# Moving the regroup copies of a fused attention and feed-forward kernel from GpSimd to ScalarE, with the sums around them rescheduled

## The chip, the cores and the metric

The kernel runs on one core of a Trainium2 chip. The metric is the device time of one execution in microseconds (us). The engines are named as the profile names them: PE is TensorE (matmuls; PEld is its loading of weights), DVE is VectorE, ACT is ScalarE, POOL is GpSimd, SP is SyncE, which here only starts stores. Each engine works through its own instructions in the order of the program and waits where an operand or a buffer isn't ready.

## What is computed

Linear attention over 8 batches of 8 heads, 576 positions and 64 features, without softmax, then an RMS norm over each head's 64 features, then a feed-forward layer with PReLU over the 4608 tokens of 512 features.

```python
kv  = einsum('bhsd,bhse->bhde', k, v)
out = einsum('bhsd,bhde->bhse', q, kv)
out = out / sqrt(mean(out*out, axis=-1, keepdims=True) + 1e-6) * g_norm
x   = out.transpose(0, 2, 1, 3).reshape(4608, 512)
h   = x @ w_in                                   # 512 -> 2048
g   = maximum(h, 0) + alpha * minimum(h, 0)
y   = g @ w_out                                  # 2048 -> 512
```

## The kernel before

The 4608 tokens are nine windows of 512, w = 0 to 8. Window 0 is worked through alone, its attention first and then its h matmuls. In **stage two** the first three quarters of window 0's output, in the banks ya, yb and yc, are accumulated beside the attention of window 1 (yc only half). After that comes one **block** for each window w from 1 to 8: its h matmuls, the output products of window w - 1, and the attention of window w + 1, in 16 units u = 0 to 15. An **epilogue** computes the products of window 8.

From window 1 on, `g @ w_out` is split into 2 x 2 quarters and done in seven products instead of eight (Strassen's method in Winograd's form). This needs sums of quarters of g (`s_sum`, 16 for each window, on DVE) and of w_out (`w_sum`, 8 in all, on DVE).

```python
def w_sum(n, i):                      # i = 0, 1: half of the rows
    ...
    else:                             # n == 3 overwrites part of w_out itself
        nc.vector.tensor_sub(
            out=w_lo(i, HC, D_MODEL), in0=w_hi(i, HC, D_MODEL), in1=w_lo(i, HC, D_MODEL))

def s_sum(w, n, k):                   # k = 0..3; needs the g groups of both halves
    t = sum_p.tile([P, 2, HW], FP16, name=f"s{n}", tag=f"s{n}{k}", bufs=1 if n == 2 else 2)
    if n == 1:   nc.vector.tensor_add(out=t[:], in0=a21, in1=a22)
    elif n == 2: nc.vector.tensor_sub(out=t[:], in0=sums[w, 1, k][:], in1=a11)
    elif n == 3: nc.vector.tensor_sub(out=t[:], in0=a11, in1=a21)
    else:        nc.vector.tensor_sub(out=t[:], in0=a12, in1=sums[w, 2, k][:])
```

q and k of a batch are loaded into a staging tile (`qst`, `kst`, two buffers each, filled by DMAs that POOL starts) with head outermost. A **regroup** copy puts them into an order (`qsb`, `ksb`, three buffers) in which the 128 columns of a head pair lie together, as PE's weight load reads them. v is read from its staging tile directly.

```python
def regroup(b, nm, h0, h1, eng=None):
    dst = bufs[b % NBUF][nm][:, 0:TPP, h0:h1, :].rearrange("p t h d -> p h t d")
    src = stages[b, nm][:, h0:h1, :, :]
    if eng is nc.scalar: nc.scalar.copy(out=dst, in_=src)
    else: (eng or nc.vector).tensor_copy(out=dst, in_=src)
```

The attention of a window goes by head pair j = 0 to 3 in four steps: `t` transposes q on PE and ACT copies it out (`qt_sb`); `kv` multiplies k and v on PE and DVE copies it out under a mask (`kv_sb`); `ot` multiplies both on PE and ACT squares it (`sq_sb`); `ssq` sums the squares on PE, ACT takes the reciprocal root (`rstd`), and DVE scales the result to `xt`, the input of the h matmuls. From block 1 on, `qt_ps`, `kv_ps` and `ssq_ps` take turns in one PSUM bank, tag "s".

The h matmuls go to two PSUM banks in turn (three before block 1). ACT takes the negative part (`m_sb`), then DVE forms g (`gt`), and only then is the bank free for the second group after it.

```python
def m1_group(w, g):
    h_ps = h_bank()
    m1_mm(h_ps, w, g, range(NC))                 # 4 matmuls of 128 x 512
    # m1_evac:
    nc.scalar.activation(out=m_sb[:], in_=h_ps[:], func=AF.Relu, scale=-1.0)
    nc.vector.scalar_tensor_tensor(out=gts[w, i][:, r, :], in0=m_sb[:],
        scalar=beta_sb[:, g:g+1], in1=h_ps[:], op0=ALU.mult, op1=ALU.add)
```

The block loop:

```python
Y_ORDER = (1, 6, 2, 7, 5, 4, 3)                  # the seven products, 16 matmuls each
PER = 7                                          # products' matmuls in a unit
Y_READS = {2: ("p1",), 5: ("u2",), 7: ("c11",), 9: ("u3",), 12: ("c22",), 14: ("c21",)}

def unit_sums(w, u):
    k, r = divmod(u, 4)
    if k > 0:
        s_sum(w, r + 1, k - 1)                   # 12 in block w, 4 in block w + 1

# t, kv, ot, ssq of pair j at units 3j, 3j + 1, 3j + 3, 3j + 5

for w in range(1, NW):
    shift = 1 if w == 1 else 0
    if w + 2 < B: load_batch(w + 2)
    for u in range(NF):
        m1_group(w, G_ORDER[u])
        unit_sums(w, u)
        if w > 1 and u < 4: unit_sums(w - 1, NF + u)
        if w == 2 and u in (1, 2): w_sum(3, u - 1)
        if w == 1 and u in (1, 3): w_sum(2 if u == 1 else 4, 1)
        if w + 2 < B and u in (10, 12):
            regroup(w + 2, "k" if u == 10 else "q", 0, H, nc.gpsimd)
        if w == 1 and u in (0, 1):
            regroup(2, "k" if u == 0 else "q", 0, H, nc.vector)
        if w > 2 and u == 0: y_read(w - 2, "c12")
        if w == 1:
            ...                                  # rest of yc (8 matmuls), and yd (16)
        else:
            for i in range(u * PER, (u + 1) * PER): prod_mm(w - 1, *Y_LIST[i])
            for what in Y_READS.get(u, ()): y_read(w - 1, what)
        attention(w + 1, u - shift)
```

The products accumulate in the banks X, Y and Z. `y_read` empties them, on ACT (p1, c11) or DVE (the others); c22 empties bank Z before the last product, n = 3, starts in it in unit 13.

Of the kernel before, what the change touches and what calls it, by code (L numbers as in the profile page):

```python
# [10 lines left out]
FP16 = mybir.dt.float16  # L11
# [6 lines left out]
def kernel(  # L18
# [11 lines left out]
    nc = tc.nc  # L30

    B, H, S, D = q.shape
    N_TOK, D_MODEL = out.shape
    D_FF = moe_w_in.shape[1]

    P = 128
    NPAIR = H // 2
    W = 512
    NW = N_TOK // W
# [5 lines left out]
    NF = D_FF // P  # L45
# [11 lines left out]
    sum_p = ctx.enter_context(tc.tile_pool(name="sums", bufs=2))  # L57
# [17 lines left out]
            name=nc.get_next_instruction_name(),  # L75
# [24 lines left out]
    for nm, src in (("q", q), ("k", k), ("v", v)):  # L100
        rem0[nm] = ysb_p.tile([P, H, D], FP32, name=f"rem0{nm}", tag="y_sb")
        nc.sync.dma_start(
            out=rem0[nm][0:REM], in_=src[0, :, MAIN:S, :].rearrange("h s d -> s h d"),
# [12 lines left out]
    bufs = []  # L116
    for i in range(NBUF):
        t = {}
        for nm in ("k", "v", "q"):
            n = 1 if nm == "v" else NT  # L120
# [21 lines left out]
# [3 lines that stand above are left out]
        if eng is nc.scalar:  # L145
            nc.scalar.copy(out=dst, in_=src)
        else:
            (eng or nc.vector).tensor_copy(out=dst, in_=src)  # L148
# [3 lines left out]
            load_rem(b, nm)  # L152
            load_main(b, nm, 0, H)

    def regroup_batch(b):
        for nm in ("k", "q"):
            regroup(b, nm, 0, H, nc.gpsimd)


    WQ = 4  # L160
# [1 line left out]
    w_out_sb = []  # L162
# [40 lines left out]
    def keep_warm(n):  # L203
# [7 lines left out]
        out=alpha_ps[:], lhsT=alpha_row[:], rhs=ident[0:NF, 0:NF], is_transpose=True,  # L211
# [5 lines left out]
        out=beta_sb[:], in0=alpha_ps[:], scalar1=-1.0, scalar2=1.0, op0=ALU.mult, op1=ALU.add,  # L217
# [107 lines left out]
    h_turn = [0]  # L325
# [33 lines left out]
    def y_mm(y, w, a, g):  # L359
        nc.tensor.matmul(  # L360
            out=y[:], lhsT=gt_cols(w, g, a * P, (a + 1) * P), rhs=w_out_blk(g),
            start=(g == 0), stop=(g == NF - 1),
        )
# [21 lines left out]
    def y_out(y, w, a):  # L385
        y_sb = ysb_p.tile([P, D_MODEL], FP32, name="y_sb")
        nc.scalar.copy(out=y_sb[:], in_=y[:])
        store_rows(w * W + a * P, y_sb[:], 0, D_MODEL)


    HC = D_MODEL // 2
    NK = NF // 2
    KQ = NK // 2
    wsum = {}

    def w_lo(i, c0, c1):
        return w_out_sb[i][:, :, c0:c1]

    def w_hi(i, c0, c1):
        return w_out_sb[i + WQ // 2][:, :, c0:c1]  # L400

    def w_sum(n, i):
        sl = slice(i * GW, (i + 1) * GW)
        if n != 3 and n not in wsum:
            wsum[n] = w_p.tile([P, NK, HC], FP16, name=f"wsum{n}")
        if n == 1:
            nc.vector.tensor_sub(
                out=wsum[1][:, sl, :], in0=w_lo(i, HC, D_MODEL), in1=w_lo(i, 0, HC)
            )
        elif n == 2:  # L410
            nc.vector.tensor_sub(
                out=wsum[2][:, sl, :], in0=w_hi(i, HC, D_MODEL), in1=wsum[1][:, sl, :]
            )
        elif n == 4:
            nc.vector.tensor_sub(
                out=wsum[4][:, sl, :], in0=w_hi(i, 0, HC), in1=wsum[2][:, sl, :]
            )
        else:
            nc.vector.tensor_sub(
                out=w_lo(i, HC, D_MODEL), in0=w_hi(i, HC, D_MODEL), in1=w_lo(i, HC, D_MODEL),  # L420
            )

    sums = {}
    HW = W // 2

    def s_sum(w, n, k):
        lo, hi = gts[w, k], gts[w, k + KQ]
        a11, a21 = lo[:, :, 0:HW], lo[:, :, HW:W]
        a12, a22 = hi[:, :, 0:HW], hi[:, :, HW:W]
        t = sum_p.tile([P, 2, HW], FP16, name=f"s{n}", tag=f"s{n}{k}", bufs=1 if n == 2 else 2)  # L430
        sums[w, n, k] = t
        if n == 1:
            nc.vector.tensor_add(out=t[:], in0=a21, in1=a22)
        elif n == 2:
            nc.vector.tensor_sub(out=t[:], in0=sums[w, 1, k][:], in1=a11)
        elif n == 3:
            nc.vector.tensor_sub(out=t[:], in0=a11, in1=a21)  # L437
        else:
            nc.vector.tensor_sub(out=t[:], in0=a12, in1=sums[w, 2, k][:])  # L439
# [20 lines left out]
    def prod_mm(w, n, i):  # L460
        a, c = divmod(i, NK)
        bank, fresh = y_bank(w, {1: "X", 2: "X", 6: "Y", 7: "Y", 4: "Y", 5: "Z", 3: "Z"}[n], a)
        cols = slice(a * P, (a + 1) * P)
        hi_cols = slice(HW + a * P, HW + (a + 1) * P)
        k, r = divmod(c, 2)
        if n == 1:
            lhs = gts[w, k][:, r, cols]
        elif n == 2:
            lhs = gts[w, k + KQ][:, r, cols]
        elif n == 4:  # L470
            lhs = gts[w, k + KQ][:, r, hi_cols]
        else:
            lhs = sums[w, {6: 2, 7: 3, 5: 1, 3: 4}[n], k][:, r, cols]
        q, rr = divmod(c, GW)
        if n == 1:
            rhs = w_out_sb[q][:, rr, 0:HC]
        elif n == 2:
            rhs = w_out_sb[q + WQ // 2][:, rr, 0:HC]
        elif n == 3:
            rhs = w_out_sb[q + WQ // 2][:, rr, HC:D_MODEL]  # L480
        elif n == 7:
            rhs = w_out_sb[q][:, rr, HC:D_MODEL]
        else:
            rhs = wsum[{4: 4, 5: 1, 6: 2}[n]][:, c, :]
        nc.tensor.matmul(  # L485
            out=bank, lhsT=lhs, rhs=rhs, start=fresh, stop=(c == NK - 1), skip_group_check=True,
        )
# [80 lines left out]
    for g in range(3, NF):  # L568
# [6 lines left out]

    AHEAD = 3
    SPLIT = 8
    ys = [
        ps_y.tile([P, W], FP32, name="ya", tag="y"),
        ps_h.tile([P, W], FP32, name="yb", tag="h0"),  # L580
# [1 line left out]
    ]  # L582
    steps = window_steps(1)
    n = len(steps)
    T_AT = {9: (1, 0), 11: (1, 1), 13: (2, 0), 15: (4, 0)}
    total = 2 * NF + SPLIT
    done = 0
    for g in range(NF):
        for a in range(AHEAD if g < SPLIT else AHEAD - 1):
            y_mm(ys[a], 0, a, g)  # L590
            done += 1
            if steps and n - len(steps) < n * done // (total - 4):
                steps.pop(0)()
        if g in T_AT:
            w_sum(*T_AT[g])
    while steps:
        steps.pop(0)()
    for a in range(AHEAD - 1):
        y_out(ys[a], 0, a)
    h_tags[0] = ("h0", "h1")  # L600
    ssq_pool[0] = (ps_s, "s")

    def unit_sums(w, u):
        k, r = divmod(u, 4)
        if k > 0:
            s_sum(w, r + 1, k - 1)

    ATT_AT = {}
    for j in range(NPAIR):
        for what, at in (("t", 0), ("kv", 1), ("ot", 3), ("ssq", 5)):  # L610
            ATT_AT.setdefault(3 * j + at, []).append((what, j))
    ATT = {"t": step_t, "kv": step_kv, "ot": step_ot, "ssq": step_ssq}

    def attention(w, u):
        if w < NW:
            for what, j in ATT_AT.get(u, ()):
                if w < B or what in ("ot", "ssq"):
                    ATT[what](w, j)

    for w in range(1, NW):  # L620
        shift = 1 if w == 1 else 0
        if w + 2 < B:
            load_batch(w + 2)
        for u in range(NF):
            m1_group(w, G_ORDER[u])
            unit_sums(w, u)
            if w > 1 and u < 4:
                unit_sums(w - 1, NF + u)
            if w == 2 and u in (1, 2):
                w_sum(3, u - 1)  # L630
            if w == 1 and u in (1, 3):
                w_sum(2 if u == 1 else 4, 1)
            if w + 2 < B and u in (10, 12):
                regroup(w + 2, "k" if u == 10 else "q", 0, H, nc.gpsimd)
            if w == 1 and u in (0, 1):
                regroup(2, "k" if u == 0 else "q", 0, H, nc.vector)
            if w > 2 and u == 0:
                y_read(w - 2, "c12")
            if w == 1:
                if u == 0:  # L640
                    yd = ps_y.tile([P, W], FP32, name="yd", tag="y")
                if u < NF - SPLIT:
                    y_mm(ys[2], 0, 2, SPLIT + u)
                    if u == NF - SPLIT - 1:
                        y_out(ys[2], 0, 2)
                y_mm(yd, 0, AHEAD, u)
                if u == NF - 1:
                    y_out(yd, 0, AHEAD)
            else:
                for i in range(u * PER, (u + 1) * PER):  # L650
                    prod_mm(w - 1, *Y_LIST[i])
                for what in Y_READS.get(u, ()):
                    y_read(w - 1, what)
            attention(w + 1, u - shift)
    w = NW - 1
    store_engines[0] = (nc.sync, nc.scalar)
    for u in range(NF):
        if u < 4:
            unit_sums(w, NF + u)
        if u == 0:  # L660
            y_read(w - 1, "c12")
        for i in range(u * PER, (u + 1) * PER):
            prod_mm(w, *Y_LIST[i])
            if i == len(Y_LIST) - NK - 1:
                y_read(w, "c12", (0,))
        for what in Y_READS.get(u, ()):
            y_read(w, what)
# [31 lines left out]
```

## Time and profile before

| | |
|---|---|
| median of 3 runs | 318.96 us (318.09 to 319.35) |
| span of the profiled run | 318.3 us |
| mean granted PE clock | 0.966 |
| window 0 | 0 to 37 us |
| stage two | 37 to 52.6 us |
| block 1 | 52.6 to 83.7 us |
| blocks 2 to 8 | first product at 83.7, 117.9, 151.9, 186.3, 216.5, 246.8, 274.8 us |
| epilogue | from 300.8 us |

The costliest groups of instructions of the kernel, by line, are the h matmuls (L335, 576 of them, 149.7 us busy), DVE's gt (L346, 144, 107.1 us) and ACT's m_sb (L342, 144, 85.9 us). The ten POOL copies (L148) take about 1.9 us each. A line of the timeline has the start, the duration, the engine, the line of the kernel, the operation, output and inputs, and in brackets how long the engine had been idle and what it had waited for. PE's matmuls overlap, so their listed durations are longer than their share of time: a 512-column matmul starts 0.215 us after the one before, a 256-column one 0.109 us.

### The profile page before, as it was taken

What the parts mean: (1) busy time and instruction counts of PE and PEld (TensorE: products, weight loads), DVE (VectorE), ACT (ScalarE), POOL (GpSimd) and SP (SyncE); (2) the same over time, 40 slices, a digit from 0 to 9 for tenths busy, and PEclk for the clock granted to TensorE, in tenths of its full rate; (3) what the DMA queues carried; (4) which work ended last, traced back from release to release, by engine and by line L of the source; (5) the groups of instructions that cost most, each with busy time, mean ns of one, the idle gap of its engine ahead of it and who ended that gap; (6) DMA issues with size and microseconds to landing.
All of it is one profiled execution on the core that took longest, in us unless ns stands there. A gap on an engine that the chain in (4) does not pass through costs nothing.

```text
span 318.3 us, 5127 instructions
## 1 busy us (share of the span) xinstructions
PE 290.4 (91%) x1972; PEld 182.7 (57%) x1972; DVE 231.7 (73%) x419; ACT 160.2 (50%) x268; POOL 62.9 (20%) x72
## 2 busy tenths in 40 slices
PE   5778897799899799997999699999999999999993
PEld 1433353354466456674666466667666666666682
DVE  4367836488788886788777787788778788876841
ACT  2246555277567435662566345755655566434310
POOL 8434333254230550054002310000000000000000
PEclk9699999799999979997999899999999999999999
DMA  7999999939981868148902920112001200210123
GB/s 106 181 206 195 201 197 193 218 48 111 149 83 35 98 92 133 34 53 124 150 0 37 162 66 10 33 35 68 2 34 35 66 17 18 67 33 33 55 80 98
DMA packets 52552, 28.32 MB, mean 89 GB/s; under 512 B 15136, under 2 KB 52016, under 8 KB 52528
## 3 DMA queue, kind: packets, MB, share of 16 engines
q0 software_dynamic: 40320, 18.16, 45.7%
q1 hardware_dynamic: 11424, 9.19, 10.2%
q10 hardware_dynamic: 784, 0.66, 0.8%
q8 instruction: 15, 0.25, 0.3%
q14 instruction: 9, 0.07, 0.1%
HBM read 36.71 MB, written 9.44 MB: 145 GB/s over the span
## 4 chain that ended last, share of the span: by engine, by line
PE 78%; DVE 11%; ACT 5%; DMA 2%; issue 2%; SPq 1%; DVEq 0%
PE h_ps L335 34%; PE yY L485 12%; PE yZ L485 9%; PE yX L485 8%; DVE gt L346 4%; PE qt_ps L236 3%; PE kv_ps L254 3%; ACT m_sb L342 3%; PE ssq_ps L293 3%; PE ot_ps L277 2%; DMA alpha_row<-in_moe_alpha_dram 2%; DVE xt L303 2%; ACT rstd L295 1%; PE yc L360 1%; DVE s L439 1%
## 5 line engine op out<-in xcount | busy, mean ns | idle before, releaser
L335 PE MATMUL h_ps<-xt,w_in_sb 128*128 128x512 f16 x576 | 149.7, 385 | 4.4 <-DVE xt L303 2.1
L346 DVE SCALAR_TENSOR_TENSOR gt<-m_sb,beta_sb,h_ps 128x512 f16<-128x512 f32 x144 | 107.1, 745 | 55.5 <-ACT m_sb L342 53.4
L342 ACT ACTIVATE m_sb<-h_ps 128x512 f32<-128x512 f32 x144 | 85.9, 597 | 93.4 <-PE h_ps L335 73.9
L335 PEld LDWEIGHTS <-w_in_sb 128*128 128x128 f16 x576 | 54.9, 99 | 52.2 <-issue 10.4
L485 PEld LDWEIGHTS <-s 128*128 128x128 f16 x512 | 51.1, 100 | 29.2 <-issue 9.8
L485 PEld LDWEIGHTS <-gt 128*128 128x128 f16 x384 | 37.6, 98 | 16.4 <-issue 1.8
L485 PE MATMUL yX<-w_out_sb,gt 128*128 128x256 f16 x256 | 35.1, 273 | 0.0
L295 ACT ACTIVATE rstd<-ssq_ps,eps_t 128x512 f32<-128x512 f32 x36 | 24.8, 689 | 18.9 <-PE ssq_ps L293 18.9
L303 DVE SCALAR_TENSOR_TENSOR xt<-ot_ps,g2col,rstd 128x512 f16<-128x512 f32 x36 | 26.8, 745 | 6.4 <-ACT rstd L295 6.3
L283 ACT ACTIVATE sq_sb<-ot_ps 128x512 f16<-128x512 f32 x36 | 21.3, 597 | 15.7 <-PE ot_ps L277 15.5
L485 PE MATMUL yZ<-w_out_sb,s 128*128 128x256 f16 x128 | 19.9, 297 | 7.0 <-DVE y_sb L512 6.9
L248 ACT COPY qt_sb<-qt_ps 128x576 f16<-128x576 f16 x28 | 17.8, 636 | 7.5 <-PE qt_ps L236 7.4
L439 DVE TENSOR_TENSOR s<-gt,s 128x512 f16<-128x512 f16 x32 | 20.6, 642 | 0.0
L131 POOL DMA_DIRECT2D vst<-in_v_dram x9 | 7.7, 858 | 64.2 <-PE kv_ps L254 60.8
L485 PE MATMUL yY<-w_out_sb,s 128*128 128x256 f16 x128 | 18.7, 272 | 0.1
L236 PE MATMUL qt_ps<-ident,qsb 128*128 128x128 f16 x160 | 15.2, 234 | 2.9 <-DVE qsb L148 2.8
L485 PE MATMUL yY<-wsum,s 128*128 128x256 f16 x128 | 17.7, 273 | 0.0
L485 PE MATMUL yY<-wsum,gt 128*128 128x256 f16 x128 | 17.6, 273 | 0.0
L485 PE MATMUL yZ<-wsum,s 128*128 128x256 f16 x128 | 17.6, 273 | 0.0
L437 DVE TENSOR_TENSOR s<-gt 128x512 f16<-128x512 f16 x32 | 17.4, 545 | 0.0
L293 PE MATMUL ssq_ps<-sq_sb,mask 128*128 128x512 f16 x36 | 14.6, 406 | 2.1 <-ACT rstd L295 1.1
L254 PEld LDWEIGHTS <-ksb 128*128 128x128 f16 x160 | 12.1, 102 | 5.7 <-issue 2.6
(65 smaller groups left out, 247.1 us busy)
## 6 DMA issues: line engine op xcount, KB each, us to landing
out_dram<-y_sb SPq DMA_DIRECT2D x72, 64.0 KB, 2.1
kst<-in_k_dram POOLq DMA_DIRECT2D x7, 512.0 KB, 8.3
qst<-in_q_dram POOLq DMA_DIRECT2D x7, 512.0 KB, 8.4
vst<-in_v_dram POOLq DMA_DIRECT2D x7, 512.0 KB, 6.1
out_dram<-y_sb SPq DMA_DIRECT2D x23, 128.0 KB, 2.0
w_in_sb<-in_moe_w_in_dram POOLq DMA_DIRECT2D x4, 512.0 KB, 14.5
w_out_sb<-in_moe_w_out_dram POOLq DMA_DIRECT2D x4, 512.0 KB, 16.6
out_dram<-y_sb SPq DMA_DIRECT2D x4, 256.0 KB, 5.9
```

The costliest lines, as they stand in the source:

```text
L236: nc.tensor.matmul(out=qt_ps[:, t * P : (t + 1) * P], lhsT=qs(t), rhs=ident16[:], is_transpose=True, start=(t == 0), stop=(t == NT - 1),)
L248: nc.scalar.copy(out=qts[b, j][:], in_=qt_ps[:, 0:S])
L254: nc.tensor.matmul(out=kv_ps[:], lhsT=ks(t), rhs=vs(t), start=(t == 0), stop=(t == NT - 1),)
L283: nc.scalar.activation(out=sq[:], in_=ot_ps[:], func=AF.Square)
L293: nc.tensor.matmul(out=ssq_ps[:], lhsT=mask16[:], rhs=sq[:], start=True, stop=True)
L295: nc.scalar.activation(out=rstd[:], in_=ssq_ps[:], func=AF.Abs_reciprocal_sqrt, bias=eps_t[:], scale=inv_d,)
L303: nc.vector.scalar_tensor_tensor(out=xts[w, j][:], in0=ot_ps[:], scalar=g2col[:], in1=rstd[:], op0=ALU.mult, op1=ALU.mult,)
L335: nc.tensor.matmul(out=h_ps[:], lhsT=w_in_blk(c, g), rhs=xts[w, c][:], start=(c == 0), stop=(c == NC - 1),)
L342: nc.scalar.activation(out=m_sb[:], in_=h_ps[:], func=AF.Relu, scale=-1.0)
L346: nc.vector.scalar_tensor_tensor(out=gts[w, i][:, r, :], in0=m_sb[:], scalar=beta_sb[:, g : g + 1], in1=h_ps[:], op0=ALU.mult, op1=ALU.add,)
L439: nc.vector.tensor_sub(out=t[:], in0=a12, in1=sums[w, 2, k][:])
L485: nc.tensor.matmul(out=bank, lhsT=lhs, rhs=rhs, start=fresh, stop=(c == NK - 1), skip_group_check=True,)
```

## The change

The change moves the regroup copies and reschedules what stands around them.

- Batches 3 to 7 are regrouped by ACT instead of POOL, in eight copies a batch, one for each head pair of q and of k, in units 8 to 15 of the block before that in which they are used.
- Batch 2 is regrouped by ACT, pair by pair, in units 0 to 6 of block 1 instead of by DVE in two copies, and the attention steps of block 1 get a plan of their own (kv in units 1 to 4, t from unit 4 on).
- The 16 sums of a window are spread over its own block (6) and the next (10), instead of 12 and 4. The number of buffers follows: two for n = 1 and 2, one for n = 3 and 4.
- Six of the eight w_out sums are done in stage two (four before) and the two of n = 3 in block 1. Those two go to a tile of their own, where before they overwrote w_out in block 2.
- Four of yc's matmuls (FILL) move from block 1 to the end of stage two, the two reads of stage two's banks change places, and block 1 begins with bank h1.

It is for freeing DVE and PE from what POOL's copies cause, and for a smooth start of block 1.

```diff
-    def regroup_batch(b):
-        for nm in ("k", "q"):
-            regroup(b, nm, 0, H, nc.gpsimd)
+    def regroup_pair(b, nm, j):
+        regroup(b, nm, 2 * j, 2 * j + 2, nc.scalar)
 ...
-        if n != 3 and n not in wsum:
+        if n not in wsum:
 ...
-                out=w_lo(i, HC, D_MODEL), in0=w_hi(i, HC, D_MODEL), in1=w_lo(i, HC, D_MODEL),
+                out=wsum[3][:, sl, :], in0=w_hi(i, HC, D_MODEL), in1=w_lo(i, HC, D_MODEL),
 ...
-        t = sum_p.tile(... bufs=1 if n == 2 else 2)
+        t = sum_p.tile(... bufs=2 if n < 3 else 1)
 ...
-    T_AT = {9: (1, 0), 11: (1, 1), 13: (2, 0), 15: (4, 0)}
+    T_AT = {5: (1, 0), 7: (1, 1), 9: (2, 0), 11: (4, 0), 13: (2, 1), 15: (4, 1)}
 ...
-    for a in range(AHEAD - 1):
-        y_out(ys[a], 0, a)
+    y_out(ys[1], 0, 1)
+    y_out(ys[0], 0, 0)
+    for g in range(SPLIT, SPLIT + FILL):
+        y_mm(ys[2], 0, 2, g)
     h_tags[0] = ("h0", "h1")
+    h_turn[0] = 0
 ...
+    S_AT = {                      # unit: (window - w, n, k)
+        0: ((-1, 1, 3),), 1: ((-1, 2, 3),), 2: ((-1, 3, 0),), 3: ((-1, 3, 1), (-1, 3, 2)),
+        4: ((-1, 3, 3),), 6: ((0, 1, 0), (0, 2, 0)), 7: ((-1, 4, 0),), 8: ((-1, 4, 1),),
+        9: ((-1, 4, 2),), 10: ((-1, 4, 3),), 11: ((0, 1, 1),), 12: ((0, 2, 1),),
+        13: ((0, 1, 2), (0, 2, 2)),
+    }
     def unit_sums(w, u):
-        k, r = divmod(u, 4)
-        if k > 0:
-            s_sum(w, r + 1, k - 1)
+        for back, n, k in S_AT.get(u, ()):
+            if 1 <= w + back < NW:
+                s_sum(w + back, n, k)
 ...
+    ATT_1 = {}
+    for j in range(NPAIR):
+        for what, at in (("kv", 1 + j), ("t", 4 + 2 * j), ("ot", 6 + 2 * j), ("ssq", 8 + 2 * j)):
+            ATT_1.setdefault(at, []).append((what, j))
 ...
-            for what, j in ATT_AT.get(u, ()):
+            for what, j in (ATT_1 if w == 2 else ATT_AT).get(u, ()):
 ...
+    REG_2 = {0: (("k", 0), ("k", 1)), 1: (("k", 2), ("k", 3))}
+    REG_2.update({3 + j: (("q", j),) for j in range(NPAIR)})
+    REG_AT = {8 + 2 * j + i: ((nm, j),) for j in range(NPAIR) for i, nm in ((0, "q"), (1, "k"))}
 ...
-            if w > 1 and u < 4:
-                unit_sums(w - 1, NF + u)
-            if w == 2 and u in (1, 2):
-                w_sum(3, u - 1)
-            if w == 1 and u in (1, 3):
-                w_sum(2 if u == 1 else 4, 1)
-            if w + 2 < B and u in (10, 12):
-                regroup(w + 2, "k" if u == 10 else "q", 0, H, nc.gpsimd)
-            if w == 1 and u in (0, 1):
-                regroup(2, "k" if u == 0 else "q", 0, H, nc.vector)
+            if w == 1 and u in (9, 15):
+                w_sum(3, 0 if u == 9 else 1)
 ...
             if w == 1:
+                for nm, j in REG_2.get(u, ()):
+                    regroup_pair(2, nm, j)
 ...
-            attention(w + 1, u - shift)
+            attention(w + 1, u)
+            if w + 2 < B:
+                for nm, j in REG_AT.get(u, ()):
+                    regroup_pair(w + 2, nm, j)
```

More of the change, by code (lines that the diff above doesn't have):

```diff
@@ L429, in s_sum @@
         a12, a22 = hi[:, :, 0:HW], hi[:, :, HW:W]
-        t = sum_p.tile([P, 2, HW], FP16, name=f"s{n}", tag=f"s{n}{k}", bufs=1 if n == 2 else 2)
+        t = sum_p.tile([P, 2, HW], FP16, name=f"s{n}", tag=f"s{n}{k}", bufs=2 if n < 3 else 1)
         sums[w, n, k] = t
@@ L480, in prod_mm @@
             rhs = w_out_sb[q + WQ // 2][:, rr, HC:D_MODEL]
-        elif n == 7:
-            rhs = w_out_sb[q][:, rr, HC:D_MODEL]
         else:
-            rhs = wsum[{4: 4, 5: 1, 6: 2}[n]][:, c, :]
+            rhs = wsum[{4: 4, 5: 1, 6: 2, 7: 3}[n]][:, c, :]
         nc.tensor.matmul(
@@ L577 @@
     SPLIT = 8
+    FILL = 4
     ys = [
@@ L615, in attention @@
         if w < NW:
-            for what, j in ATT_AT.get(u, ()):
+            for what, j in (ATT_1 if w == 2 else ATT_AT).get(u, ()):
                 if w < B or what in ("ot", "ssq"):
                     ATT[what](w, j)
+    REG_2 = {0: (("k", 0), ("k", 1)), 1: (("k", 2), ("k", 3))}
+    REG_2.update({3 + j: (("q", j),) for j in range(NPAIR)})
+    REG_AT = {8 + 2 * j + i: ((nm, j),) for j in range(NPAIR) for i, nm in ((0, "q"), (1, "k"))}
     for w in range(1, NW):
-        shift = 1 if w == 1 else 0
         if w + 2 < B:
@@ L639 @@
             if w == 1:
+                for nm, j in REG_2.get(u, ()):
+                    regroup_pair(2, nm, j)
                 if u == 0:
                     yd = ps_y.tile([P, W], FP32, name="yd", tag="y")
-                if u < NF - SPLIT:
-                    y_mm(ys[2], 0, 2, SPLIT + u)
-                    if u == NF - SPLIT - 1:
+                g = SPLIT + FILL + u
+                if g < NF:
+                    y_mm(ys[2], 0, 2, g)
+                    if g == NF - 1:
                         y_out(ys[2], 0, 2)
@@ L657 @@
     for u in range(NF):
-        if u < 4:
-            unit_sums(w, NF + u)
+        unit_sums(NW, u)
         if u == 0:
```

## The prediction

> **What bounds the kernel now.** I began with the page: busy time by engine, then the slices. PE, the matmul engine, is busy for 91% of the span, no other engine for more than 73%. Where PE is dense nothing else can matter, so the question is where it is not.
>
> ```profile
> PE 290.4 (91%) x1972; PEld 182.7 (57%) x1972; DVE 231.7 (73%) x419; ACT 160.2 (50%) x268; POOL 62.9 (20%) x72
> ...
> PE   5778897799899799997999699999999999999993
> ...
> POOL 8434333254230550054002310000000000000000
> PEclk9699999799999979997999899999999999999999
> ```
>
> A slice is 8 us. After the start PE has dips, the granted clock falls to 7 tenths in the same slices, and the dips end when POOL's work ends. The table by stretches says what a dip costs. I cut the span where the first product of a block (yX) starts: 83.74, 117.86 and so on. Each row is start:end, length, then busy time of PE, PEld, DVE, ACT, POOL, then granted clock.
>
> ```profile
> 52.58:83.74 31.16, 26.75 (x145) 12.79 (x144) 23.92 (x42) 17.33 (x30) 11.14 (x10) 0.95 1.07 141
> 83.74:117.86 34.12, 32.04 (x229) 21.19 (x228) 27.50 (x45) 17.88 (x30) 12.12 (x12) 0.95 0.60 81
> 117.86:151.86 34.00, 31.91 (x230) 21.24 (x229) 26.98 (x46) 17.88 (x30) 8.75 (x9) 0.95 0.59 87
> 151.86:186.29 34.43, 31.91 (x229) 21.17 (x228) 26.80 (x46) 17.88 (x30) 6.33 (x6) 0.95 0.54 80
> 186.29:216.54 30.25, 30.24 (x230) 20.45 (x228) 23.76 (x46) 17.88 (x30) 0.00 (x0) 1.00 0.13 37
> ```
>
> The last four rows hold the same work (block 2 has two w_out sums more). With POOL idle it takes 30.25 us, PE wholly busy at full clock. With POOL working it takes 34.0 to 34.4 us, and DVE is busy 3 us longer for 45 or 46 instructions in each row. The timeline round the end of block 2 shows why (start, duration, engine, line; in brackets the idle time before and who ended it).
>
> ```profile
> 106.52 2.68 DVE L439 TENSOR_TENSOR s<-gt,s 128x512 f16<-128x512 f16 x1
> ...
> 106.98 1.92 POOL L148 COPY ksb<-kst 128x2048 f16<-128x2048 f16 x1
> ...
> 110.78 0.68 DVE L512 TENSOR_TENSOR y_sb<-yZ,u 128x512 f32<-128x512 f32 x1
> ...
> 111.50 0.38 PE L485 MATMUL yZ<-w_out_sb,s 128*128 128x256 f16 x2 [2.08 <-DVE y_sb L512]
> 111.50 0.10 PEld L485 LDWEIGHTS <-s 128*128 128x128 f16 x1 [2.26 <-issue]
> 111.61 0.71 PEld L335 LDWEIGHTS <-w_in_sb 128*128 128x128 f16 x4
> 111.72 1.51 PE L335 MATMUL h_ps<-xt,w_in_sb 128*128 128x512 f16 x4
> ```
>
> The sum s takes 2.68 us, where its median is 0.42; a POOL regroup copy lies inside it. DVE works in order, so the read c22 that must empty bank yZ comes late, and PE waits 2.08 us for it. Then the clock is down: the next four h matmuls take 1.34 us on the chain of waits instead of 0.86, and the seven yZ after them 1.49 instead of 0.76. The list of waits has this one four times, and the same shape sits at 145.6 and 180.1.
>
> ```profile
> PE yZ L485 <- DVE y_sb L512: 6.9, 4, 2.5
> ```
>
> Block 1 (52.58 to 83.74) has its own holes. PE idles 0.94 us before it, for ACT's reads of stage two's banks; 2.25 us at 57.58, for DVE's regroup of batch 2's q, followed by slow matmuls to 61; 1.31 us at 83.52, for DVE's xt; and some 0.3 us three times behind small ops.
>
> **What the Trainium skill says.** "GPSIMD Engine Reference", section 8 (Key points), says that GpSimd shares its SBUF interfaces with VectorE and contends with VectorE instructions that have two SBUF inputs. The trace agrees: the stretched instructions under a POOL copy are the sums s with two SBUF inputs, up to 3.12 us; the gt and xt ops, which read PSUM, stay at 0.75.
> "TensorE: Matmul & The Clock Gate", Part 1, says that idleness of about one 3.4 us window brings half clock. Here gaps of 2.08 and 2.25 us were already followed by slow matmuls, so a gap costs more than its length.
> "VectorE: DVE Perf Modes", section on the TRN2 errata, gives ScalarE 224 cycles plus one per element at 1.2 GHz from SBUF to SBUF. My estimate from it for a head-pair copy of 512 elements is 0.613 us. The trace's ACT casts of 512 elements from SBUF took 0.614 to 0.618, over half the partitions.
>
> **The change part by part.**
> 1. *Regroup of batches 3 to 7 leaves POOL for ACT.* Ten POOL copies of 1.9 us go; forty ACT copies of about 0.6 us come, eight in each of blocks 1 to 5. What goes is the stretching. In blocks 2, 3 and 4 that is worth 34.12 + 34.00 + 34.43 - 3 x 30.25 = 11.8 us.
> What comes is ACT load. An ACT instruction that follows directly starts about 0.5 us after the one before (81.03 to 81.52 to 81.99), so eight copies add about 4 us to ACT's 17.9 busy us in a block of 30.25. They all sit in units 8 to 15. There ACT has, at durations as listed, 8 m (4.8), 3 rstd (2.1), 2 sq (1.2), 1 qt (0.6) and 8 copies (4.8): 13.5 us. PE has, per unit, four h matmuls (0.86) and seven products (0.77), in eight units 13.0, plus one transposition, one kv, two ot and three ssq, 1.6 together: 14.7. So ACT fits, barely: the worst unit is 9, with m, sq, qt and a copy. Two h banks give each m some 1.6 us of room before PE must wait.
> But c22 has no room: in block 5, undisturbed, it ends at 211.94 and its yZ starts at 211.99, some 0.2 us after the product before it was through. A copy ahead of m in unit 12 delays gt and then c22 by about 0.2. I charge 0.3 us to each of blocks 2 to 5: +1.2.
> 2. *Batch 2 pair by pair on ACT, attention of block 1 in a new order, FILL.* Two DVE copies of 0.69 us go; eight ACT copies come in units 0 to 6. Four matmuls of bank yc (4 x 0.215 = 0.86 us) move ahead of block 1 and cover the wait for the two reads; block 1 begins with bank h1, free by then. That 0.94 us should go. The 2.25 us hole should go too, with its slow matmuls (about 1.5 us), since q's first pair is wanted only in unit 4. In exchange ACT carries block 1: 16 m, 16 copies, 4 sq, 2 reads of y at about 0.5, 4 qt and 4 rstd at 0.6: 23.8 us, beside 22 us for PE (84 x 0.215 + 3.95 for attention). Both are near full, and the one bank "s" serves kv, qt and ssq in turn. I walked it unit by unit: PE idles about 1.3 us in unit 4 (kv waits for ACT's qt in bank s), 0.8 in unit 8 and 1.0 in unit 10 (t waits for rstd), and block 2's first product starts at about 79.5 instead of 83.74: -4.2 us. It uses q of batch 3 at about 68; the trace has it landing at 67.2, so that transfer is just in time.
> 3. *Sums spread over two blocks; w_out sums earlier, the fourth in a tile of its own.* The count stays: 16 sums a block, 8 w_out sums. They only move: block 1 gives up six sums, the epilogue gains six on an idle DVE; two w_out sums of 0.68 us go from block 1 to stage two, where DVE is busy 7.7 of 15.6 us, and the two of n = 3 from block 2 to block 1. The worth is in not standing before kv, xt and c22; I count no further gain.
> 4. *Loads.* q and k of a later batch are taken up when ACT has freed the staging buffer rather than POOL. The regroup of a batch stands a block ahead of its use, and the DMA column above falls from 1.07 in block 1 to 0.54 in block 4: hidden.
>
> Sum: -11.8 + 1.2 - 4.2 = -14.8, from 318.96: 304.2. My walk of block 1 assumes each wait ends at its earliest, so I add a little: **304.5 us**.
>
> **The rivals.**
> *ACT becomes the bound.* For: in units 8 to 15 it is at nine tenths, in block 1 it is above PE, and m is what frees PE's banks. Were a copy 0.75 us instead of 0.6, units 8 to 15 would be full and each of blocks 2 to 5 would lose 1 to 2 us, block 1 two or three: 311. Against: one after the other ACT ops overlap by 0.1 us, and units 0 to 7 let it catch up.
> *A wait takes the place of the one removed.* c22 remains the tight spot; batch 3's q may land late and hold ACT, in order, with m behind it. A wait of 2 us there also lowers the clock: +2 to +4, so 307 to 308.
> *DVE was only the messenger and PE gets little.* Then blocks 2 to 4 would stay at 34 and the time near 314. Against: block 5 has the same work without POOL and takes 30.25.
> *Better than said.* If block 1 ran at PE's 22 us plus 2, it would save 3 us more: 301.5.
>
> **Range and chances.** The 11.8 us are read from the trace and I trust them to 2 us; block 1 to 3 us either way; ACT's backlog can cost up to 6. That gives 301.5 to 308.5. Within 2% begins at 312.6, which needs the first rival at its worst; slower needs something unseen.
>
> **What would show it.** In the profile after: no POOL copy; the L439 and L437 sums at 0.42 with no long maximum; blocks 2 to 5 each at 30.3 to 30.8 us, clock 1.00; ACT busy about 22.5 in each, the copies at 0.6; block 2's first product near 79.5. Wrong would be: blocks over 31.5 with PE waiting for gt (ACT bound), block 1 beyond 82, ACT waiting for q or k of a batch, or clock dips that stay.

## The result, and the profile after

The changed kernel takes **303.68 us** (median; 303.47 to 303.83), beside 319.15 us for the kernel before in the same session. The ratio is 0.9504, with a 95% interval of 0.9447 to 0.956. The prediction was 304.5 us with a range of 301.5 to 308.5.

The page of the changed kernel, the lines that answer to those shown of before:

```profile
PE 281.4 (93%) x1972; PEld 179.5 (59%) x1972; DVE 220.6 (73%) x417; ACT 181.4 (60%) x316; POOL 44.1 (15%) x62
...
PE   5678899889899999999999999999999999999993
...
POOL 8434424340200420042003000000000000000000
PEclk9799999999999999999999999999999999999998
```

PE's dips and the falls of the clock in the middle of the span are gone. ACT has 21 us more to do, POOL 19 less (what is left on it starts loads), and PE is 9 us less busy with the same 1972 matmuls: 5.35 us of that lie in blocks 2 to 4, where none of them runs at a low clock any more.

The table by stretches, cut where the first product of a block starts: stretch, length, busy time of PE, PEld, DVE, ACT and POOL, granted clock. The last two columns are DMA.

```profile
52.00:79.08 27.08, 23.78 (x140) 11.76 (x139) 18.52 (x33) 24.08 (x47) 6.25 (x8) 1.00 1.31 173
79.08:109.50 30.42, 30.18 (x230) 20.56 (x228) 24.18 (x46) 21.78 (x39) 4.69 (x6) 1.00 0.61 84
109.50:139.92 30.42, 30.17 (x230) 20.61 (x229) 24.01 (x46) 21.45 (x38) 4.72 (x6) 1.00 0.64 94
139.92:170.33 30.41, 30.16 (x229) 20.56 (x228) 24.00 (x46) 21.45 (x38) 4.01 (x5) 1.00 0.59 92
170.33:200.75 30.42, 30.17 (x230) 20.46 (x228) 24.01 (x46) 21.45 (x38) 0.00 (x0) 1.00 0.14 42
200.75:230.93 30.18, 30.17 (x229) 20.35 (x228) 24.08 (x46) 17.88 (x30) 0.00 (x0) 1.00 0.11 33
```

Blocks 2, 3 and 4 take 30.4 us each instead of 34.0 to 34.4. Block 5, which had no POOL copy before either, is 0.17 us longer than its 30.25 before. That is not all that ACT's copies cost: block 6, which has none, takes 30.18, and so does block 5 of the run e2 below, which has none on any engine. ACT's copies cost 0.24 us a block, and the new plan of the sums gives back 0.07. From the first product of block 2 to that of block 5 the kernel before took 186.29 - 83.74 = 102.55 us and this one 170.33 - 79.08 = 91.25: **11.3 us**. The first product of block 2 starts at 79.08 instead of 83.74. Stage two's first matmul had started 0.5 us earlier (36.58 against 37.09), which is the start of the run and not the change; so stage two and block 1 are worth **4.1 us**.

Where DVE's sums had been stretched, the groups by tile now show no long maximum (duration in ns: minimum, median, maximum). First the two with the longest before, then the four now:

```profile
L437 DVE TENSOR_TENSOR s<-gt x32: 412/418/1778, 68.1 to 303.0; 128x512 f16<-128x512 f16 x32
L439 DVE TENSOR_TENSOR s<-gt,s x32: 409/418/3116, 70.6 to 303.3; 128x512 f16<-128x512 f16 x32
```
```profile
L432 DVE TENSOR_TENSOR s<-gt x32: 414/418/424, 64.4 to 285.3; 128x512 f16<-128x512 f16 x32
L434 DVE TENSOR_TENSOR s<-s,gt x32: 414/422/426, 64.8 to 286.2; 128x512 f16<-128x512 f16 x32
L436 DVE TENSOR_TENSOR s<-gt x32: 415/418/419, 84.4 to 287.6; 128x512 f16<-128x512 f16 x32
L438 DVE TENSOR_TENSOR s<-gt,s x32: 415/418/420, 94.0 to 292.2; 128x512 f16<-128x512 f16 x32
```

PE's own idle times in the timeline, from block 1 on (start, duration, in brackets the idle time before and who ended it):

```profile
60.65 0.38 PE L253 MATMUL kv_ps<-vst,ksb 128*128 128x128 f16 x4 [1.20 <-ACT qt_sb L247]
66.95 0.44 PE L235 MATMUL qt_ps<-ident,qsb 128*128 128x128 f16 x5 [0.61 <-ACT rstd L294]
70.71 0.44 PE L235 MATMUL qt_ps<-ident,qsb 128*128 128x128 f16 x5 [0.73 <-ACT rstd L294]
76.75 1.02 PE L334 MATMUL h_ps<-xt,w_in_sb 128*128 128x512 f16 x4 [0.54 <-DVE gt L345]
78.21 1.04 PE L334 MATMUL h_ps<-xt,w_in_sb 128*128 128x512 f16 x4 [0.22 <-DVE gt L345]
104.95 0.38 PE L482 MATMUL yZ<-w_out_sb,s 128*128 128x256 f16 x2 [0.24 <-DVE y_sb L509]
```

The first three are waits for the shared bank "s" in block 1, the next two are for gt, and the last is the wait for c22, 2.08 us before, 0.24 now. It comes again in blocks 3, 4 and 5 (0.25 each) and 8 (0.23).

### The profile page after: what moved, and what is told of

It reads as the page before. It is cut to its first block, busy times and chain, and to the rows that moved or that the text cites. A ratio compares the mean times of both kernels' runs of the same rounds, so it can differ in the third digit from the quotient of the medians.

```text
span 302.0 us, 5167 instructions
## 1 busy us (share of the span) xinstructions
PE 281.4 (93%) x1972; PEld 179.5 (59%) x1972; DVE 220.6 (73%) x417; ACT 181.4 (60%) x316; POOL 44.1 (15%) x62
## 3 DMA queue, kind: packets, MB, share of 16 engines
q1 hardware_dynamic: 11424, 9.19, 10.6%
## 4 chain that ended last, share of the span: by engine, by line
PE 78%; ACT 7%; DVE 4%; DMA 4%; issue 3%; POOL 2%; DVEq 0%; POOLq 0%
PE h_ps L334 35%; PE yY L482 12%; PE yZ L482 10%; PE yX L482 9%; DMA w_in_sb<-in_moe_w_in_dram 4%; ACT m_sb L341 3%; PE qt_ps L235 3%; PE kv_ps L253 3%; PE ssq_ps L292 2%; PE ot_ps L276 2%; DVE gt L345 2%; ACT ksb L146 1%; ACT rstd L294 1%; PE yc L359 1%; DVE y_sb L509 1%
## 5 line engine op out<-in xcount | busy, mean ns | idle before, releaser
L334 PE MATMUL h_ps<-xt,w_in_sb 128*128 128x512 f16 x576 | 146.0, 379 | 3.4 <-DVE gt L345 2.3
L334 PEld LDWEIGHTS <-w_in_sb 128*128 128x128 f16 x576 | 54.1, 98 | 49.8 <-issue 5.5
L482 PEld LDWEIGHTS <-s 128*128 128x128 f16 x512 | 50.1, 98 | 21.6 <-issue 2.5
L482 PEld LDWEIGHTS <-gt 128*128 128x128 f16 x384 | 37.6, 98 | 14.8
L482 PE MATMUL yY<-wsum,s 128*128 128x256 f16 x256 | 36.3, 273 | 0.0
L482 PE MATMUL yZ<-w_out_sb,s 128*128 128x256 f16 x128 | 17.5, 272 | 1.2 <-DVE y_sb L509 1.2
L235 PE MATMUL qt_ps<-ident,qsb 128*128 128x128 f16 x160 | 14.4, 225 | 2.1 <-ACT rstd L294 1.3
L292 PE MATMUL ssq_ps<-sq_sb,mask 128*128 128x512 f16 x36 | 13.6, 379 | 1.4 <-ACT rstd L294 1.1
L146 ACT COPY qsb<-qst 128x512 f16<-128x512 f16 x24 | 14.8, 617 | 0.0
L146 ACT COPY ksb<-kst 128x512 f16<-128x512 f16 x24 | 14.8, 624 | 0.0
L235 PEld LDWEIGHTS <-qsb 128*128 128x128 f16 x160 | 11.2, 100 | 5.5 <-issue 2.2
## 6 DMA issues: line engine op xcount, KB each, us to landing
kst<-in_k_dram POOLq DMA_DIRECT2D x7, 512.0 KB, 13.8
```

The costliest lines, as they stand in the source:

```text
L235: nc.tensor.matmul(out=qt_ps[:, t * P : (t + 1) * P], lhsT=qs(t), rhs=ident16[:], is_transpose=True, start=(t == 0), stop=(t == NT - 1),)
L292: nc.tensor.matmul(out=ssq_ps[:], lhsT=mask16[:], rhs=sq[:], start=True, stop=True)
L334: nc.tensor.matmul(out=h_ps[:], lhsT=w_in_blk(c, g), rhs=xts[w, c][:], start=(c == 0), stop=(c == NC - 1),)
L482: nc.tensor.matmul(out=bank, lhsT=lhs, rhs=rhs, start=fresh, stop=(c == NK - 1), skip_group_check=True,)
```

## The experiments

**What the copies were worth alone, and by which way.** Theory A: a POOL copy holds up DVE's sums, c22 comes late, PE waits, its clock falls. Rivals: the new plan of sums or of block 1 carries the gain (B), or slow copies brought PE's operands late (C).

*e1, copies only.* The kernel before, with

```diff
-            if w + 2 < B and u in (10, 12):
-                regroup(w + 2, "k" if u == 10 else "q", 0, H, nc.gpsimd)
+            if w + 2 < B and u >= 8:      # after attention(...)
+                j, i = divmod(u - 8, 2)
+                regroup(w + 2, "qk"[i], 2 * j, 2 * j + 2, nc.scalar)
```

> The kernel before with one thing changed: batches 3 to 7 are regrouped on ACT, eight copies a batch in units 8 to 15. Theory A (GpSimd's copies stretch DVE's sums, that delays c22, PE waits and its clock falls): blocks 2, 3 and 4 fall from 34.0 to 34.4 us to 30.3 to 30.8, block 1 moves by under 1 us, the time is 307 to 309. Rival B (the new plan of the sums or of block 1 carries the gain): blocks 2 to 4 stay over 32.5, the time is 313 or more.

Measured: 308.7 us (306.69 to 310.09), ratio 0.9648 (0.9597 to 0.9699). Two of its blocks in the table by stretches:

```profile
81.22:111.69 30.47, 30.23 (x229) 20.56 (x228) 23.59 (x45) 21.45 (x38) 4.69 (x6) 1.00 0.63 86
111.69:142.17 30.48, 30.23 (x229) 20.63 (x228) 23.73 (x46) 21.46 (x38) 4.72 (x6) 1.00 0.66 95
```

The move of the copies alone brings blocks 2 to 4 to 30.5 us. Block 1 keeps its 2.25 us hole and its wait for xt (1.27 us). Rival B falls for blocks 2 to 4. The trace is that of the fastest of the four runs.

*e2, POOL's copies back.* The changed kernel, with the eight ACT copies replaced by the two POOL copies of before, in units 10 and 12.

> The changed kernel with batches 3 to 7 regrouped by GpSimd again, in whole copies in units 10 and 12; the rest of the change stays. Theory A: blocks 2 to 4 back to 33.5 to 34.5 us with long sums beside the copies, the time is 313 to 316. Rival B (spread sums give DVE the room it needs): blocks 2 to 4 at 30.3 to 31, the time is 305 or less, since ACT is spared 4 us a block.

*e4, copies that nobody reads.* The changed kernel as it is, plus

```diff
+            if w + 2 < B and u in (10, 12):
+                nc.gpsimd.tensor_copy(
+                    out=scratch[:].rearrange("p t h d -> p h t d"),
+                    in_=stages[w + 2, "k" if u == 10 else "q"][:])
```

To find room for `scratch`, the fourth w_out sum is written in place again.

> The changed kernel, regroup on ACT as it is, and besides ten GpSimd copies of the staging tiles into a tile that nobody reads, in units 10 and 12. Nothing waits for their result. Theory A (contention for SBUF with DVE): sums stretched to 2 us and more, blocks 2 to 4 at 33 to 34.5 us, the time is 312 to 316. Rival C (what mattered was that PE's operands came late from a slow GpSimd): blocks as in the changed kernel, 30.4, the time is 304.

Measured: e2 312.39 us (311.56 to 313.64; ratio 0.9772, 0.9732 to 0.9811), e4 314.43 us (313.55 to 316.97; ratio 0.9845, 0.9792 to 0.9898). The timeline of e4 at the end of block 2:

```profile
102.25 2.68 DVE L433 TENSOR_TENSOR s<-gt 128x512 f16<-128x512 f16 x1
...
102.71 1.92 POOL L672 COPY scratch<-kst 128x2048 f16<-128x2048 f16 x1
...
106.50 0.68 DVE L512 TENSOR_TENSOR y_sb<-yZ,u 128x512 f32<-128x512 f32 x1
...
107.23 0.39 PE L485 MATMUL yZ<-w_out_sb,s 128*128 128x256 f16 x2 [2.08 <-DVE y_sb L512]
```

Nothing waits for what this copy writes, and yet the picture of the kernel before is back, to the 2.08 us. So it is contention between POOL's copy and a sum on DVE, and not a late operand: rival C falls. The spread plan of the sums doesn't protect from it; another sum stands there and is stretched instead, to as much as 3.11 us in e4 and 3.12 in e2. The stretched sum ends 0.3 us after the copy does: it is in effect held until the copy is over.

Theory A's figures came true for e4. For e2 they came true in block 4 only (34.26 us); blocks 2 and 3 take 32.25 and 32.26, and the time stays under the 313 expected. Blocks 2, 4 and 5 of e2, then block 2 of e4:

```profile
79.52:111.77 32.25, 30.17 (x229) 20.57 (x228) 27.11 (x46) 17.88 (x30) 10.52 (x10) 1.00 0.64 88
...
144.03:178.29 34.26, 31.74 (x229) 21.10 (x228) 26.55 (x46) 17.88 (x30) 8.12 (x8) 0.95 0.56 81
178.29:208.47 30.18, 30.17 (x229) 20.44 (x228) 23.89 (x45) 17.88 (x30) 0.00 (x0) 1.00 0.13 38
```
```profile
79.53:113.46 33.93, 31.85 (x230) 21.11 (x229) 27.35 (x46) 21.45 (x38) 10.96 (x10) 0.95 0.63 86
```

In block 2 PE waited the same 2.08 us in both. In e2 the clock stayed at 1.00 and the block is 30.17 us of work and 2.08 of wait. In e4 the clock fell to 0.95 and PE needed 31.85 us for the same matmuls: 1.68 us more. The loss is short and deep: in the 3.42 us that follow the wait the granted clock was 0.54 in e4 and 1.00 in e2. So the 3.8 us that block 2 or 3 of the kernel before lost were 2.1 of wait and 1.7 of clock, and the second part can be absent. The same holds for block 1: in the 3.42 us after the 2.25 us hole the clock was 0.51 in the kernel before, and it stayed at 1.00 after the same hole in e1.

*e3, the old plan of the sums.* The changed kernel with `unit_sums` as before (12 in the block, 4 in the next), its buffers, and the fourth w_out sum in place.

> The changed kernel with the sums of a window planned as before (12 in its block, 4 in the next) and the fourth w_out sum again in place. Theory A: blocks 2 to 5 stay at 30.3 to 30.7 us, the time is 303 to 305. Rival B (the spreading is a part of the gain): 306 or more, with PE waiting for sums or for c22.

Measured: 304.31 us (303.98 to 304.48). Blocks 2 to 5 take 30.48 us, block 7 28.01 instead of 27.94, block 8 25.85 instead of 25.57. The spread plan is worth some 0.6 us in all, of 15, and none of it in block 1: measured as below, block 1 takes 29.16 us here and 29.20 in the changed kernel. Rival B's 306 isn't reached.

**What shortened block 1.** Since runs start up to 2 us apart, block 1 is measured here from the last ssq matmul of stage two to block 2's first product: 50.40 to 83.74 = 33.34 us before, 49.88 to 79.08 = 29.20 after. Below, "the stretch" is this length. Where whole runs differ by a microsecond or so, they are also compared by their traces, from the same ssq matmul to the first product of the epilogue: 49.88 to 284.44 = 234.56 us in the changed kernel.

*e5, no fill.* `FILL = 0`, the two reads in their old order, no reset of the bank turn.

> The changed kernel without the four matmuls moved ahead of block 1, with the two reads in their old order and the bank order of before. Theory A (they cover the wait for the two reads): PE waits some 0.9 us for ACT's reads ahead of block 1, and the time is 0.5 to 1.2 us above the changed kernel's 303.7. Rival D (block 1 is bound by ACT, so a late start of PE costs nothing): no difference, within 0.4 us.

Measured: 304.55 us (303.75 to 304.95). PE waits 0.94 us for ACT's read ahead of block 1, and the stretch is 30.10 us, 0.90 longer. Theory A holds by the traces; the times of the whole runs overlap with the changed kernel's (303.75 against 303.83).

*e6, batch 2 on DVE.*

```diff
-                for nm, j in REG_2.get(u, ()):
-                    regroup_pair(2, nm, j)
+                if u in (0, 3):
+                    regroup(2, "k" if u == 0 else "q", 0, H, nc.vector)
```

> The changed kernel with batch 2 regrouped on DVE in two whole copies, k in unit 0 and q in unit 3 of block 1; the order of attention stays as changed. Theory A (in block 1 ACT carries too much, and what helped was q's later place, not ACT): eight ACT copies less, block 1 shorter by 1 to 2 us, 302 to 303. Rival E (the pairs on ACT are what makes block 1 short): block 1 longer by 1 us or more, 304.5 or more.

Measured: 303.94 us (303.67 to 304.81), the stretch 29.82 us. Neither expectation: no gain from eight ACT copies less, and a loss of 0.62 us, less than a microsecond, from leaving the pairs. PE waits in other places (0.35 for k, 0.48 and 0.73 for bank "s") and then meets the same waits in units 8 to 15. So the engine that copies batch 2 accounts for little of the 4.1 us, FILL for 0.9 (e5) and the sums for nothing (e3). What is left is that q is copied later and wanted later, in the new order of attention, and that two w_out sums have left block 1. No run takes these apart, so it is argued and not shown that q's later place is the cause.

*e7, t in a bank of its own.*

```diff
-                    ATT[what](w, j)
+                    if w == 2 and what == "t":
+                        step_t(w, j, (ps_q, "q"))
+                    else:
+                        ATT[what](w, j)
```

> The changed kernel with the transposed q of block 1 in the bank that the products use only later, so that kv, rstd and qt no longer take turns in one bank. Theory A (the PE waits of 1.2, 0.6 and 0.7 us in block 1 are waits for that bank and set its length): the waits go, block 1 is shorter by 1.3 to 2.3 us, 301.5 to 302.5. Rival D (ACT's load alone sets block 1, at 24 of 27 us busy): under 0.7 us gained, PE waits for gt instead.

Measured: 302.1 us (301.96 to 302.52), the stretch 27.63 us. The three waits of 1.20, 0.61 and 0.73 are gone; new waits for gt of 0.32 and 0.69 stand in units 8 to 15, where ACT has batch 3 as well. Both stories are right in part: 2.5 us of bank waits removed, 1.0 given back in waits for gt, which waits for ACT's m. By the traces the gain is 1.56 us.

**How tight the rest is.**

*e8, c22 ahead of a sum.* `(0, 2, 1)` moves from unit 12 to unit 13.

> The changed kernel with one sum of unit 12 moved behind c22 into unit 13. Theory A (ACT's copy and that sum ahead of c22 leave yZ waiting 0.24 us in blocks 2 to 5 and 8): the wait is gone, blocks 2 to 5 at 30.18 to 30.25 us, 302.3 to 303.3 in all. Rival: a wait of the same size for another operand, blocks as they are at 30.42.

Measured: 302.05 us (301.51 to 302.23). PE has no listed wait left after block 1; blocks 2 to 5 take 30.08 us, 0.34 gained and not 0.24. A listed wait begins at the listed end of the matmul before, which is later than the next could have started: from the five yY matmuls before yZ to yZ it was 103.99 to 104.95 in the changed kernel, 0.96 us, and is 103.59 to 104.21 here, 0.62. Block 1, where there is no c22 to gain from, gets 0.8 us longer by the same move (29.97). By the traces the whole gain is 1.26 us.

*e11, whole copies on ACT.* Two copies of 2048 elements in units 10 and 12 instead of eight of 512.

> The changed kernel with batches 3 to 7 regrouped on ACT in two whole copies a batch, in units 10 and 12, instead of eight. Theory A (an ACT copy of 1.9 us holds m for longer than the 1.6 us that two banks give, and holds c22 too): PE waits in blocks 1 to 5, these at 31.5 to 33.5 us, 308 to 314. Rival F (the cutting into pairs doesn't matter; ACT even saves start-up time, 2 x 1.9 against 8 x 0.6 us): 303 to 305.

Measured: 307.35 us (307.16 to 307.83), between the two. The copies take 1.89 us. Block 1 has waits for gt of 1.21 and 1.31 us and is 1.9 us longer; but blocks 2 to 5 take only 30.88, 0.47 more. There a unit of PE lasts 1.6 to 2.1 us, where in the second half of block 1 some last only 1.1. The two banks cover the wait for m, and c22, ahead of the q copy, is held no longer than in the changed kernel (yZ waits 0.20 us); the only new wait is 0.27 us for xt. So pairs mattered most in block 1; that the short units are the reason fits, but no run varies them.

*e12, pairs on DVE.* The same eight copies of batches 3 to 7 in the same units, on DVE.

> The changed kernel with the eight pair copies of batches 3 to 7 on DVE instead of ACT, in the same units. DVE copied 2048 elements in 0.69 us, so a pair should take about 0.3. Theory A (DVE may carry the copies as well as ACT; only GpSimd beside DVE's sums is bad): blocks 2 to 5 within 0.4 us of 30.42, 303 to 305. Rival G (DVE's order ahead of c22 and kv is the tight one and any copy there costs PE): blocks over 31, 306 or more.

Measured: 302.74 us (302.24 to 303.15), 0.9 us below the change itself by the medians and 0.7 by the traces (233.84 against 234.56 us). The line of its copies (ns: minimum, median, maximum) and, in the same form, ACT's in e9:

```profile
L148 DVE COPY ksb<-kst x23: 282/285/685, 10.8 to 199.3; 128x512 f16<-128x512 f16 x20, 128x1024 f16<-128x1024 f16 x2, 128x2048 f16<-128x2048 f16 x1
```
```profile
L146 ACT COPY ksb<-kst x24: 607/618/729, 53.3 to 197.7; 128x512 f16<-128x512 f16 x24
```

0.28 us on DVE against 0.62 on ACT; blocks 2 to 5 fall to 30.27 us, and their wait for c22 is gone. Theory A holds, with a total a little better than its 303 to 305; rival G falls.

*e9, e7 and e8 together; e10, and batch 2 on DVE.*

> The changed kernel with the transposed q of block 1 in bank Z and the sum of unit 12 behind c22. If the two gains (1.6 us each) lie in different stretches, as the traces say, they add: 300 to 301. If ACT's queue carries one into the other: 301.3 or more.

> As the run before it, and batch 2 regrouped by DVE in two whole copies. With the bank's waits gone ACT is what holds block 1 (PE waits for gt). Theory A: eight ACT copies less give block 1 another 0.5 to 1.5 us, 299 to 300.3. Rival: the waits for gt come from the second half of block 1, where the copies of batch 3 lie, so nothing or a small loss: 300.3 to 301.

Measured: e9 **301.04 us** (300.93 to 301.14; ratio to the kernel before 0.9406, 0.9336 to 0.9475), e10 **300.77** (300.49 to 301.32; 0.9398, 0.9341 to 0.9456). They beat the changed kernel by 2.6 and 2.9 us. The 301.04 of e9 lies between its two expectations, which took the gains of 1.6 from whole runs. By the traces the two gains are 1.56 and 1.26 us, and e9 gains 2.94 (231.62 against 234.56 us): they add. Its stretch is 28.29 us against 27.63 in e7. About half of that is what e8's move costs in block 1 (the last wait for gt is 0.55 us instead of 0.21); the other half stands at a wait for gt of 0.64 instead of 0.32, behind a copy of batch 3's q for which ACT waited 0.34 us on the load.

For e10 the rival holds. Its whole runs overlap with e9's, and its stretch is 28.78 us, 0.5 longer than e9's: the waits for gt of 0.28, 0.68, 0.55 and 0.55 us all stand in the second half of block 1, where batch 3 is copied.

## Why the prediction was right

Its sum was -14.8 from 318.96, and 0.3 set aside. Measured: -15.5 between the medians.

1. *POOL's copies leave: -11.8, and ACT's cost +1.2.* Measured together -11.3 in blocks 2 to 4 and +0.17 in block 5, where I had -10.6. The reading of block 5 as a block without POOL was right, and e1, e2 and e4 show the mechanism. ACT's cost was 0.24 us a block instead of 0.3, at the place named (the wait for c22; e12, without ACT's copies, has none). The net 0.17 is smaller because the new plan of the sums, for which nothing was counted, gains 0.07.
2. *The ACT copy at 0.613 us*, an estimate from "VectorE: DVE Perf Modes": measured 0.617 and 0.624 on average. ACT's busy time in blocks 3 to 5 is 21.45 us, not "about 22.5"; the prediction's own 17.9 and "about 4" make 21.9. That a following ACT instruction starts 0.1 us before the listed end of the one before is also what "ScalarE: Activation LUTs", section "What ACT_TABLE_LOAD costs", gives (93 ns); this trace has 103.33, 103.83, 104.33, 104.82 for four in a row.
3. *Block 1: -4.2.* Measured -4.1. The three PE waits that I walked to, 1.3 in unit 4, 0.8 in unit 8 and 1.0 in unit 10, came as 1.20, 0.61 and 0.73, on the operands named. The waits for gt at its end (0.54 and 0.22) I had not seen. So the close figure is partly luck: the three waits came out 0.56 us shorter together than forecast, and 0.76 us of other waits took their place. And the slow matmuls behind the hole, counted as a sure gain of about 1.5 us, are a loss that e1's traced run escaped. The step called "ACT carries block 1" was only half right: e6 took eight copies off ACT and gained nothing while the bank waits stood, and e7, without them, met waits for gt; but e10 shows that even then taking batch 2's copies off ACT doesn't shorten block 1.
4. *The sums: no further gain.* e3 shows about 0.6 us between the medians, and 0.63 by the traces (235.19 against 234.56 us): small but there.
5. *Loads hidden.* The list of waits has no ACT copy waiting for a DMA in the changed kernel, although the median time to landing of k rose from 8.3 to 13.8 us. Batch 3's q is just in time, as said: its first copy starts at 67.96. In e9, whose block 1 comes sooner, ACT waits 0.3 us for it.

The step least understood was the clock. "TensorE: Matmul & The Clock Gate", Part 1, ties the fall to about 3.4 us of idleness and says that its window runs freely. Here 2.08 us sufficed in e4 and in the kernel before, and did not in two blocks of e2. A gap of 2.08 us fills no whole window of 3.4 us, whatever its phase, so the measurement goes beyond the page: a shorter gap can be enough. In block 2 of e2 and of e4 the wait ends at the same time after the start (107.22 and 107.23 us), and only one of them lost its clock; that fits a window that isn't tied to the start of the kernel, but no run controlled its phase, so it stays open. The prediction took the loss as certain. Had the kernel before escaped it in blocks 2 to 4, the gain would have been up to 5 us smaller (three times 1.7), though none of its runs came below 318.05 us.

## What to carry to other kernels

When DVE is busier than its instruction count explains, look for a GpSimd copy inside the long ones: a copy off the critical path can hold an instruction that is on it, and the stall that follows may be paid a second time as clock. Before moving such a copy to the engine with most idle time, price it on all: here DVE, the "busy" engine, did it in less than half of ACT's time and came out 0.7 us ahead. And when several short-lived results share one PSUM bank, the bank's turns can set the pace before the engines do (here 1.56 us in block 1), so try an unused bank before shifting load from one engine to another.

## What was not expected of the hardware

- The 2.08 us wait came back to 0.01 us in two kernels with another plan of the sums. In block 2 of all three kernels POOL's copy stands behind the start of v's load, which waits for kv, and yZ starts 4.52 us after the copy does.
- The same wait of 2.08 us cost PE 1.68 us of clock in one run and nothing in another.
- A regroup copy of 128 x 512 in 16 bits took 0.28 us on DVE and 0.62 us on ACT; the one of 128 x 2048 took 0.69, 1.89 and 1.9 us on DVE, ACT and POOL.
